# Linear attention with decay and a mixture of experts: products with the state in four quarters of TensorE, two pairs of heads exchanged

## The chip, the core and the metric

The kernel runs on one core of a Trainium2 chip. The core has five engines that work side by side: TensorE (PE, matrix products; the loads of its weights are shown as PEld), VectorE (DVE), ScalarE (ACT), GpSimd (POOL) and SyncE (SP, which here only issues loads and stores). Products land in PSUM, [...] all else lies in SBUF. The metric is the device time of one execution in microseconds; less is better.

## The reference

The first part is attention with a decaying state, for 4 sequences, 8 heads, 768 positions and a head size of 64. The second sends each of the 3072 rows of its result through the one expert of eight that a gate chooses. All data are fp32.

```python
def _attn_ref(q, k, v):
    ...
    for t in range(S):
        state = gamma[None, :, None, None] * state + np.einsum('bhd,bhe->bhde', k[:, :, t], v[:, :, t])
        y[:, :, t] = scale * np.einsum('bhd,bhde->bhe', q[:, :, t], state)
    return y.astype(np.float32)

def _moe_ref(x, w_gate, w1, w2):
    logits = x @ w_gate
    expert_idx = np.argmax(logits, axis=1)
    ...
    for e in range(E):
        ...
        h = np.maximum(x_sorted[lo:hi] @ w1[e], 0.0)
        y_sorted[lo:hi] = h @ w2[e]
    y = y_sorted[inv_perm]
    return (gate_w[:, None] * y).astype(np.float32)
```

## The kernel before

**Attention.** A sequence is cut into 6 chunks of 128 positions (two chunks of a pair hold the even and odd positions' q in one load). There are 24 steps, one for each chunk `c` and sequence `b`, in the order chunk 0 and 1 of sequence 0, then of sequence 1, and so on; then chunks 2 and 3, then 4 and 5. The decay is put into q and v by factors, so that a chunk needs only plain products. The eight heads lie in four pairs `a`; the two heads `j` of a pair lie in partitions 0 to 63 and 64 to 127.

In step n, `retain` does on TensorE:

- L440, `sc`: scores, k times q, for 8 heads. The depth is 64, so a product uses half of the array's rows and all its columns; the heads `j` alternate between the upper and the lower rows and write two banks.
- VectorE multiplies the two banks by the causal mask (L442, `am`).
- `then()`: the transposes of the next step's k (L387, 4 of them) and, for every other step, of q (8 more), which ACT copies to SBUF (L425, L428); the layout change of the step before on VectorE (L476, from `xTg` to `xg`); and one piece of the routing work.
- L451, `new`: the chunk's own contribution to the state, 8 products; VectorE adds the old state (L454).
- L465, `y`: q times the old state, 8 products of depth 64 with 64 outputs, for all chunks but the first of a sequence. The heads of a pair use the two diagonal quarters of the array: rows 0 to 63 with columns 0 to 63, and rows 64 to 127 with columns 64 to 127.
- L469, `y`: masked scores times v, added in the same place in PSUM; 8 products of depth 128 with 64 outputs, so that the two heads of a pair use the left and the right half of the columns.
- ACT copies `y` to `xTg` (L471), one copy of 128 partitions by 512.

The tile `y` has two PSUM buffers, one bank each, used in turn; `tr` has three, `sc` two, `lg` one.

**Loads.** `load(n + 5)` is issued by SyncE in step n. GpSimd scales q and v two steps ahead (L399, L404).

**Routing.** After each four steps `place` works on the 512 rows that are complete: gate products (L493, `parts`), a transpose (L502), the choice and its softmax on VectorE (L504 to L523), ranks within each expert (L526 to L540), and a list of rows for each expert (L543 to L582). `place` is a generator; the steps that follow take one piece of it at a time, in an order written out by hand. [...]

**The end of attention and the experts.** After the last step the rows of the first expert that are known already are gathered (L166), copied (L643), transposed (L656) and given to its first layer (L221). Then the eight experts follow, each with a first layer (L221, ReLU by ACT at L223) and a second one, either as plain products (L234) or, for the first 256 rows, as seven instead of eight half-size products (L275, `pair`). Outputs are scattered to HBM by GpSimd (L310).

Each fp32 product of the program appears as two matrix instructions in the trace.

## Time and profile before

| | |
|---|---|
| time, median of 3 runs | 483.25 us (480.48 to 483.81) |
| span of the profiled execution | 481.1 us |
| attention on TensorE | about 10 to 133 us |
| experts on TensorE | about 138 to 473 us |
| TensorE busy | 463.0 us (96%) |
| VectorE busy | 267.0 us (55%) |
| ScalarE busy | 106.8 us (22%) |
| GpSimd busy | 136.1 us (28%) |

Busy time counts an instruction from its start to its modelled end, and overlapping ones once. A line of a group names the line of the kernel, the engine, the operation, what it writes and reads with its shape, how often, then the busy time in us, the mean time of one in ns, and the idle time of the engine before it with what ended that. In a list in order of time the first number is the start and the second the length, both in us. The chain that ended last is followed back from the last instruction, at each point to what released it.

### The profile page before, as it was taken

The numbers are of one execution on the slowest core, as the hardware profiler recorded it, in microseconds if no ns is written. First come the engines' busy times: TensorE is split into PE (matmuls) and PEld (weight loads), VectorE is DVE, ScalarE is ACT, GpSimd is POOL, SyncE is SP. The second block draws the span as 40 slices with busy tenths as digits, with TensorE's granted clock in tenths as the row PEclk, the third lists the DMA queues.
The fourth block names the chain that finished last, engine by engine and source line by source line (L and its number), as shares of the span: only waits on it lengthen the run. The fifth ranks groups of instructions, "written<-read, shape, count | busy, mean of one in ns | idle before, by whom it ended". The sixth has DMA issues, their size and how long they took to land.

```text
span 481.1 us, 8296 instructions
## 1 busy us (share of the span) xinstructions
PE 463.0 (96%) x3262; PEld 325.1 (68%) x3262; DVE 267.0 (55%) x548; ACT 106.8 (22%) x219; POOL 136.1 (28%) x134
## 2 busy tenths in 40 slices
PE   8999999999889999999999999999999999999992
PEld 4778778787668965655585558668556765755782
DVE  4468786777677891576516632583571537470320
ACT  2343333333222011122211121131122111012110
POOL 2772533541304235023017002602601331100211
PEclk9999999999989999999999999999999999999997
DMA  9999999887831099234008401920920380240011
GB/s 204 220 236 218 216 240 221 194 209 232 278 89 41 6 354 360 115 110 164 3 28 285 169 2 53 364 80 26 354 96 32 116 350 19 66 158 3 27 46 48
DMA packets 93515, 72.53 MB, mean 151 GB/s; under 512 B 53482, under 2 KB 78058, under 8 KB 93424
## 3 DMA queue, kind: packets, MB, share of 16 engines
q1 hardware_dynamic: 88160, 58.74, 42.9%
q0 software_dynamic: 5120, 12.60, 7.5%
q8 instruction: 48, 0.79, 0.7%
q14 instruction: 43, 0.35, 0.2%
q10 hardware_dynamic: 144, 0.05, 0.0%
HBM read 60.88 MB, written 14.68 MB: 157 GB/s over the span
## 4 chain that ended last, share of the span: by engine, by line
PE 86%; DVE 7%; SPq 1%; DMA 1%; ACT 1%; issue 1%; another core or an unknown queue 1%; POOL 0%; POOLq 0%; DVEq 0%; ACTq 0%
PE hp L221 34%; PE yp L275 20%; PE ye L234 12%; PE y L469 4%; PE sc L440 4%; PE tr L387 3%; PE y L465 3%; DVE xT L209 2%; PE new L451 2%; PE parts L493 1%; DMA q<-in_q_dram 1%; SPq L374 1%; DVE am L442 1%; PE lgp L502 1%
## 5 line engine op out<-in xcount | busy, mean ns | idle before, releaser
L221 PE MATMUL hp<-xTs,w1t 128*128 128x392 f32 (+5 forms) x384 | 127.4, 493 | 0.0
L221 PEld LDWEIGHTS hp<-xTs,w1t 128*128 128x128 f32 x384 | 73.1, 190 | 52.3 <-issue 29.7
L310 POOL DMA_INDIRECT out_dram<-o,dst x30 | 33.0, 1100 | 226.5 <-ACT o L242 135.7
L209 DVE STREAM_TRANSPOSE xTs<-xs 32x512 f32<-32x512 f32 x96 | 67.4, 703 | 50.6 <-DMA xs<-x_d,src 49.3
L234 PE MATMUL ye<-w2t,hT 128*8 128x128 f32 (+6 forms) x496 | 66.4, 361 | 0.0
L223 ACT ACTIVATE hT<-hp 128x392 f32<-128x392 f32 (+6 forms) x64 | 29.4, 467 | 146.5 <-PE hp L221 130.1
L234 PEld LDWEIGHTS ye<-w2t,hT 128*8 128x8 f32 (+6 forms) x496 | 32.6, 123 | 31.3 <-issue 28.8
L166 POOL DMA_INDIRECT xs<-x_d,src x28 | 38.4, 1370 | 26.5 <-DVE gate_e L201 18.2
L442 DVE TENSOR_TENSOR am<-sc,causal 128x512 f32<-128x512 f32 x48 | 30.8, 682 | 21.7 <-PE sc L440 18.3
L281 DVE SCALAR_TENSOR_TENSOR u<-yp,gate,m 128x256 f32<-128x256 f32 x14 | 6.8, 484 | 56.2 <-PE yp L275 42.2
L404 POOL TENSOR_TENSOR vs<-v,dec 128x512 f32<-128x512 f32 x23 | 24.3, 1056 | 36.3 <-PE y L469 19.9
L275 PE MATMUL yp<-ws,hs 128*128 128x256 f32 x144 | 32.1, 380 | 0.0
L275 PEld LDWEIGHTS yp<-ws,hs 128*128 128x128 f32 x144 | 27.4, 190 | 3.7
L399 POOL TENSOR_TENSOR qs<-q,dec 128x512 f32<-128x512 f32 x22 | 22.6, 1046 | 23.6 <-DMA q<-in_q_dram 22.6
L469 PE MATMUL y<-am,vs 128*64 128x128 f32 x384 | 27.7, 279 | 1.5 <-DVE am L442 1.4
L440 PE MATMUL sc<-qT,kT 64*128 64x128 f32 x384 | 27.9, 285 | 0.7 <-ACT kT L425 0.7
L275 PE MATMUL yp<-w2t,hT 128*128 128x256 f32 x112 | 26.6, 380 | 0.0
L440 PEld LDWEIGHTS sc<-qT,kT 64*128 64x128 f32 x384 | 23.3, 187 | 4.6 <-issue 3.6
L469 PEld LDWEIGHTS y<-am,vs 128*64 128x64 f32 x384 | 21.2, 137 | 5.9 <-issue 3.3
L275 PEld LDWEIGHTS yp<-w2t,hT 128*128 128x128 f32 x112 | 21.2, 190 | 5.3 <-issue 2.8
L471 ACT COPY xTg<-y 128x512 f32<-128x512 f32 x24 | 14.1, 585 | 46.2 <-PE y L469 42.1
L221 PE MATMUL hp<-xTa,w1t 128*128 128x256 f32 (+1 forms) x128 | 22.1, 330 | 0.7 <-ACT xTa L658 0.7
(188 smaller groups left out, 543.1 us busy)
## 6 DMA issues: line engine op xcount, KB each, us to landing
w1t<-in_moe_w_dram SPq DMA_DIRECT2D x8, 2048.0 KB, 13.7
w2t<-in_moe_w_dram SPq DMA_DIRECT2D x8, 2048.0 KB, 11.6
k<-in_k_dram SPq DMA_DIRECT2D x24, 256.0 KB, 5.5
v<-in_v_dram SPq DMA_DIRECT2D x24, 256.0 KB, 5.7
x_d<-xg SPq DMA_DIRECT2D x24, 256.0 KB, 4.9
q<-in_q_dram SPq DMA_DIRECT2D x11, 512.0 KB, 5.5
q<-in_q_dram SPq DMA_DIRECT2D x2, 256.0 KB, 3.3
out_dram<-o,dst POOLq DMA_INDIRECT x30, 3.3
```

Of the source, the lines that this page charges most:

```text
L166: nc.gpsimd.indirect_dma_start(out=xs[:, t, :], out_offset=None, in_=x_d[0:rows, :], in_offset=bass.IndirectOffsetOnAxis(ap=idx[:, t : t + ...
L209: nc.vector.transpose(xT[ts(g, L), :, 0 : n * P].rearrange("p a (t r i) -> p r t a i", r=Q, i=L)[:, r, :, :, :], xs[ts(r, L), tiles[0] : t ...
L221: nc.tensor.matmul(hp, lhsT=w1t[:, 0, dt, ts(f, P)], rhs=xT[:, dt, 0:n], start=(dt == 0), stop=(dt == DT - 1))
L223: nc.scalar.activation(out=hT[:, f, 0:n], in_=hp, func=AF.Relu)
L234: nc.tensor.matmul(y[j * z : j * z + m, 0:c], lhsT=hT[:, f, t * P + r0 : t * P + r0 + m], rhs=w2t[:, 0, f, ts(j, c)], start=(f == 0), stop ...
L275: nc.tensor.matmul(y, lhsT=a[:, f, :], rhs=b[:, f, :], start=start and f == 0, stop=f == FH - 1, skip_group_check=True)
L310: done = nc.gpsimd.indirect_dma_start(out=out[:, :], out_offset=bass.IndirectOffsetOnAxis(ap=idx[:, t : t + 1], axis=0), in_=o[:, t, :], i ...
L399: mul.tensor_tensor(out=qs[:, e, part, :], in0=got["q"][:, part, ts(e, D)], in1=inner(dec[:, ts(c + e, H)][:, part], D), op=ALU.mult)
L404: mul.tensor_tensor(out=vs, in0=got["v"], in1=inner(dec[:, ts(NC + c, H)], D), op=ALU.mult)
L440: nc.tensor.matmul(sc[j][:, a, :], lhsT=kT[r, a, :], rhs=qT[r, a, :], start=True, stop=True)
L442: nc.vector.tensor_tensor(out=am[j], in0=sc[j], in1=middle(causal[:, :], HP), op=ALU.mult)
L469: nc.tensor.matmul(y[ts(j, D), a, :], lhsT=vs[:, 2 * a + j, :], rhs=am[j][:, a, :], start=(c == 0), stop=True, skip_group_check=True)
```

## The change

The exchange puts the heads of the last two pairs (a = 2, 3) on the other diagonal: the head in rows 0 to 63 writes columns 64 to 127, and the reverse. The state products of one of the first two pairs and one of the last two are issued one after the other, so that four products stand in a row that use four different quarters of the array. [...] the last two pairs have a bank of their own; both `y` buffers are now taken in each step. The second product, L469, follows the same places. The copy puts the exchanged heads back: ACT copies the first two pairs as before (128x256) and each exchanged half by itself (64x256, from the upper partitions to the lower ones and the reverse). In the last step VectorE makes these two copies.

```diff
-            y = ps("y", 2, "y").rearrange("p (a t) -> p a t", a=HP)
+
+            HB = HP // 2
+            y = [ps("y", 2, "y")[:, 0 : HB * P].rearrange("p (a t) -> p a t", a=HB) for _ in range(2)]
+            place_of = lambda a, j: y[a // HB][ts(j ^ (a // HB), D), a % HB, :]
             if c:
-                for a in range(HP):
+                for a in (0, HB, 1, HB + 1):
                     for j in range(2):
                         r = ts(j, D)
-                        nc.tensor.matmul(y[r, a, :], lhsT=old[r, a, :], rhs=qT[r, a, :], start=(a == 0), stop=False,
-                                         skip_group_check=True)
+                        nc.tensor.matmul(place_of(a, j), lhsT=old[r, a, :], rhs=qT[r, a, :], start=(a % HB == 0),
+                                         stop=False, skip_group_check=True)
             for a in range(HP):
-                for j in range(2):
-                    nc.tensor.matmul(y[ts(j, D), a, :], lhsT=vs[:, 2 * a + j, :], rhs=am[j][:, a, :], start=(c == 0),
+                for j in (range(2) if a < HB else (1, 0)):
+                    nc.tensor.matmul(place_of(a, j), lhsT=vs[:, 2 * a + j, :], rhs=am[j][:, a, :], start=(c == 0),
                                      stop=True, skip_group_check=True)
-            nc.scalar.copy(out=xTg[n // B % 2][:, :, n % B, :], in_=y)
+            x = xTg[n // B % 2][:, :, n % B, :]
+            nc.scalar.copy(out=x[:, 0:HB, :], in_=y[0])
+            for j in range(2):
+                to, got = x[ts(j, D), HB:HP, :], y[1][ts(1 - j, D), :, :]
+                if n + 1 < len(steps):
+                    nc.scalar.copy(out=to, in_=got)
+                else:
+                    nc.vector.tensor_copy(to, got)
```

## The prediction

> **What bounds the kernel now.** I read three views in this order: the page (who is busy, and the chain that ended last), the time order of one step, and VectorE's own time order around the places where its work piles up. From the page, the engine totals and the chain:

> ```profile
> PE 463.0 (96%) x3262; PEld 325.1 (68%) x3262; DVE 267.0 (55%) x548; ACT 106.8 (22%) x219; POOL 136.1 (28%) x134
> ...
> PE 86%; DVE 7%; SPq 1%; DMA 1%; ACT 1%; issue 1%; another core or an unknown queue 1%; POOL 0%; POOLq 0%; DVEq 0%; ACTq 0%
> PE hp L221 34%; PE yp L275 20%; PE ye L234 12%; PE y L469 4%; PE sc L440 4%; PE tr L387 3%; PE y L465 3%; DVE xT L209 2%; PE new L451 2%; PE parts L493 1%; DMA q<-in_q_dram 1%; SPq L374 1%; DVE am L442 1%; PE lgp L502 1%
> ```

> TensorE is 86% of the chain. The products with the state, L465, are 3%, some 15 to 20 us in the attention part (about 10 to 133 us). A microsecond saved there should reach the end: after 181 us the chain is L221, L234 and L275 in turn with no gap over 0.02 us until 472.7. One step, in time order, TensorE only (start us, us, engine, line, what):

> ```profile
> 60.66 0.66 PE L387 MATMUL tr<-ident,k 128*128 128x128 f32 x4
> 61.24 0.69 PE L451 MATMUL new<-vs,k 128*64 128x64 f32 x16
> 61.86 1.09 PE L465 MATMUL y<-qT,state 64*64 64x128 f32 x16
> 62.88 1.09 PE L469 MATMUL y<-am,vs 128*64 128x128 f32 x16
> ```

> No gap: L465 holds TensorE for 1.02 us (61.86 to 62.88), and L469 follows at once. Each product of the program is two instructions (8 give x16). Their kinds, from the groups with shapes kept apart (busy us, mean ns):

> ```profile
> L465 PE MATMUL y<-qT,state 64*64 64x128 f32 x320 | 22.1, 276 | 0.2 <-issue 0.2
> L451 PE MATMUL new<-vs,k 128*64 128x64 f32 x320 | 13.7, 228 | 0.5 <-ACT qT L428 0.5
> L234 PE MATMUL ye<-w2t,hT 128*32 128x128 f32 x128 | 3.9, 274 | 0.0
> ```

> All overlap: 276 ns each, but 22.1/320 = 69 ns apart. The third row is what the change hopes for: four tiles of the array at work at once, 128 columns streamed as in L465, and 3.9/128 = 30 ns apart.

> **How many run at once, and what a turn costs.** In the single starts of the trace L465 goes in pairs 7 ns apart, a pair every 109 ns; L234 goes in fours, one within 20 ns, a four every 109 ns. The rows agree: one burst of L465 is 22.1/20 = 1.105 us for 8 turns, one of L234 is 3.9/2 = 1.95 us for 16, so a turn is (1.95 - 1.105)/8 = 0.106 us and a burst has 0.25 us that doesn't depend on turns. I take 0.109.

> [...] L440 shows two row tiles at once, L469 two column tiles. [...] from the last start of L465 to the first of L469 is 0.20 us instead of 0.109. [...]

> **The change, part by part.**
> 1. *State products, 20 steps* (c>0, six groups of four less the first). 8 turns become 4: 20 x (8-4) x 0.109 = **8.7 us** less on TensorE. Upper price of a turn: if loading four sets of 64 weights were the limit, L451 prices it: a burst of 13.7/20 = 0.685 us, less 0.25, over 8 pairs = 0.054 per pair, so 0.109 again for four. I see no slower turn in the trace short of no overlap at all (part of the rivals).
> 2. *L469*: same 8 products, columns still alternate left, right; other banks. Nothing.
> 3. *Copies*: one ACT copy of 128x512 (585 ns) becomes one of 128x256 and two of 64x256. The nearest rows are 383 ns (the activation of 128x256) and 366 ns (L239, 64x256). The first can run beside the second half of L469, so the end of the copying moves from 0.59 to 2 x 0.37 = 0.73 us after L469; ACT is busy 0.53 us more per step, on an engine busy 8.5 of 25 us in this part. Behind them in ACT's queue stands the next kT copy, which needs L440 and the transposes first (1.09 + 0.49 = 1.6 us after L469). To L476, which reads the copies, it makes no difference: VectorE does both masks of the next step first. Nothing.
> 4. *PSUM*: both y buffers are now used in each step, so a step's first y product waits for the copies of the step before and no longer for those two back. It stands after L440, L387 and L451, at least 1.09 + 0.49 + 0.62 = 2.2 us after L469, and the copies need 0.8. Nothing; 1.4 us in hand.
> 5. *Last step*: VectorE does the two half copies, about 0.4 us each by the state row (418 ns, 128x256 out of PSUM), ahead of its copies to xe (0.72 us), while ACT copies the other half. The first two products of L493 can start earlier, the last two about 0.2 us later. I take 0; 0.3 either way for the range.

> **What keeps the 8.7 us from arriving.** L469 also needs the two masks of VectorE (L442). VectorE's time order in a step after a routing round began:

> ```profile
> 59.47 0.18 DVE L537 TENSOR_TENSOR own<-rk,ohs 128x32 f32<-128x32 f32 x1
> 59.69 0.19 DVE L540 TENSOR_REDUCE ranks<-own 128x4 int32<-128x32 f32 x1
> 59.91 0.93 DVE L543 TENSOR_SCALAR col<-ranks 128x4 int32<-128x4 int32 x1
> 60.76 0.16 DVE L544 TENSOR_SCALAR prow<-ranks 128x4 int32<-128x4 int32 x1
> 60.88 0.17 DVE L546 TENSOR_TENSOR is_col<-four,col 128x16 f32<-128x16 int32 x1
> 61.09 0.29 DVE L548 TENSOR_TENSOR at<-ohs,is_col 128x128 f32<-128x128 bf16 x1
> 61.30 1.28 DVE L442 TENSOR_TENSOR am<-sc,causal 128x512 f32<-128x512 f32 x2
> ```

> No idle time: from 53.3 (L504) to 68.8 VectorE is never free, so L442 comes when VectorE gets to it. It ends at 62.58, and L469 starts at 62.88: 0.23 us in hand, where a shorter L465 would want 0.44. [...] Going through all steps in this way (steps numbered from 0; wanted 0.44 each):
> - 1, 3, 7, 8, 11, 12, 13, 15, 16, 20, 22: L442 is done early enough. All kept.
> - 5: TensorE already waits for L442 in step 6 (40.81, 0.16 us), VectorE unbroken since 32.4. 0.44 lost.
> - 9 and 10: 0.23 kept of 0.87. 0.64 lost.
> - 14: at 88.66 TensorE waits 1.15 us for VectorE's state sum (L454), which moves only as much as its chain's start. 0.44 lost.
> - 17 to 19: L442 ends at 109.62 and L469 starts at 110.71, so about 1.03 kept of 1.31. 0.28 lost.
> - 21: the next work is L579, which needs L572, unbroken VectorE work that ends at 123.26. 0.33 lost.
> - 23: VectorE stands still from 127.50 to 130.91 before the last masks (releaser unknown to the profile); L465 is beside it. 0.44 lost.

> Lost 2.57, kept 8.7 - 2.57 = 6.1: **483.25 - 6.1 = 477.1 us**.

> Loads don't take it back: the load queue is full up to 88 us, but then waits for buffers that TensorE frees; the last v load is issued at 96.8 and lands about 5.7 us later (median), while its scaling starts at 111.95. That and all weights (w1: issued 104.3, 13.7 us to land, used at 138) have over 9 us in hand.

> **Rivals.**
> - *B, VectorE gives way too.* The piled-up stretches start when TensorE gives the routing its input[...]; if they fall elsewhere, all 8.7 arrive: 474.5. For: VectorE is busy 18.2 us of the 25 from 50 to 75 us, no full engine. Against: the unbroken stretches above.
> - *C, the quarters don't overlap fully*, because two row tiles share the output columns: 8 turns stay, 483.3. For: this trace has no four-way burst with two row tiles. Against: L440 and L234 each show half of it.
> - *D, slower: changing between the two diagonals costs a drain*[...]. Eight turns stay and three changes inside each burst cost 0.20 - 0.109, about 0.1 us each: 20 x 0.3 = 6.0, 489.2. For: the 0.20 us gap.[...]

> **How the numbers follow.** Chances: forecast 0.61, B 0.16, C 0.15, D 0.08. One per cent is 4.8 us (below 478.4). The forecast misses that in about one case of seven (its losses could be 4 us), so faster 0.52 + 0.16 = 0.68, slower 0.08, the rest same. Low end: B, less 1.5 us because L493 took 1.94 us at the reduced clock after the standstill at 130 (about 1.0 us in the earlier rounds) and L656 lost about as much; the clock may stay full: 473.0. High end 481.5: the forecast with losses doubled (479.7) and the spread of the times before (480.5 to 483.8, 1.8 us of it). D and most of C stay outside.

> **What would show it.** L465's successor at about 4 x 0.109 + 0.25 = 0.69 us per burst (13.7 us busy in all, from 22.1) and 0.58 us from its start to that of the next products; starts in fours. New waits of TensorE for L442 of 1 to 3 us in all. No wait of TensorE for ACT's y copies. If the burst stays at 1.0 us, C; above 1.2, D. If the burst is short and the waits for L442 are under 0.5 us, B.

## The result, and the profile after

| | before | changed |
|---|---|---|
| time, median (5 runs each, side by side) | 483.81 us (480.48 to 485.37) | 478.5 us (477.54 to 479.73) |
| ratio to before, 95% interval | | 0.990 (0.9856 to 0.9944) |
| span of the profiled execution | 481.1 us | 475.8 us |

The changed kernel takes 5.3 us less by the medians, and 5.3 us less by the two spans; by the interval the saving is 2.7 to 7.0 us. In the experiments further down, a run more than 1.5% above the fastest of its kernel counts as slow and is left out of the medians and ranges. From here on the lines of the changed kernel are meant where it is spoken of: L468 are its products with the state (L465 before), L472 the masked ones (L469), L475 and L479 ScalarE's copies (L471), L481 VectorE's two copies of the last step, L486 the layout change (L476). All of the routing stands ten lines lower than before.

The page of the changed kernel, engine totals and chain:

```profile
PE 456.0 (96%) x3262; PEld 316.9 (67%) x3262; DVE 267.2 (56%) x550; ACT 118.5 (25%) x265; POOL 135.9 (29%) x134
...
PE 83%; DVE 7%; DMA 4%; SPq 1%; issue 1%; ACT 1%; another core or an unknown queue 1%; POOL 0%; POOLq 0%; DVEq 0%; ACTq 0%
PE hp L221 34%; PE yp L275 20%; PE ye L234 12%; PE y L472 4%; PE sc L440 3%; DMA w2t<-in_moe_w_dram 3%; PE tr L387 3%; PE new L451 2%; PE y L468 2%; DVE am L442 2%; PE parts L503 1%; DMA q<-in_q_dram 1%; SPq L374 1%; PE lgp L512 1%
```

TensorE is 7.0 us less busy with the same 3262 instructions, and the products with the state fall from 3% of the chain to 2%. VectorE's masks, L442, rise from 1% to 2%: part of the gain meets them. ScalarE has 46 instructions more and 11.7 us more to do. The new 3% of a load of second-layer weights (w2t) is hardly a loss: at 175 us TensorE waits 1.1 us for it, where before it waited 0.95 us for VectorE.

The same kernel, TensorE, time order of the step that was shown of before (start us, us, engine, line, what), and the groups of this part with shapes kept apart:

```profile
57.08 0.66 PE L387 MATMUL tr<-ident,k 128*128 128x128 f32 x4
57.66 0.69 PE L451 MATMUL new<-vs,k 128*64 128x64 f32 x16
58.28 0.67 PE L468 MATMUL y<-qT,state 64*64 64x128 f32 x16
58.87 1.09 PE L472 MATMUL y<-am,vs 128*64 128x128 f32 x16
```

```profile
L472 PE MATMUL y<-am,vs 128*64 128x128 f32 x384 | 29.5, 285 | 1.3 <-DVE am L442 1.2
L468 PE MATMUL y<-qT,state 64*64 64x128 f32 x320 | 13.8, 282 | 1.9 <-issue 1.2 <-remote 0.7
L451 PE MATMUL new<-vs,k 128*64 128x64 f32 x320 | 13.7, 228 | 0.5 <-ACT qT L428 0.5
```

One product takes as long as before (282 ns against 276), but the sixteen now hold TensorE for 0.67 us instead of 1.09, and L472 starts 0.60 us after L468 (58.28 to 58.87) instead of 1.02. So the gain is overlap, not shorter instructions. The last row is a control: L451 was not touched, and kept its 13.7 us and 228 ns. L472 has 29.5 us, L469 had 27.7: the last burst of L472 takes 2.48 us, while the granted clock of TensorE is 0.5 (from 125.5 to 128.9 us). The trace of before has such a stretch too, from 133.7 to 137.1 us, so the two traces are alike in this.

The waits of TensorE in the attention part, 10 to 135 us (engine, line, waited for: us in total, times, longest), changed kernel:

```profile
PE y L472 <- DVE am L442: 1.2, 3, 0.8
PE y L468 <- issue: 1.2, 1, 1.2
PE tr L387 <- DVE state L454: 1.2, 1, 1.2
PE tr L387 <- POOL qs L399: 0.8, 2, 0.4
PE y L468 <- remote: 0.7, 1, 0.7
PE hp L221 <- ACT xTa L668: 0.7, 1, 0.7
PE found L589 <- DVE here L582: 0.6, 1, 0.6
```

In the trace of before the waits for masks came to 1.4 us, 1.2 of them in the last step. The total says little, then; what is new is 1.0 us in step 17.

**Where the time went.** The start of the masked products, compared step by step between the two traces, tells how far the changed kernel is ahead. It starts 0.69 us ahead in step 0, which the change did not bring: up to 7.4 us the first transposes of q on TensorE (L387) follow each other after 0.21 us in the trace of before, and after 0.11 us here. The loads landed alike (the first scaling of q starts at 4.05 and 4.04 us).

```
step                1     5     8     9    14    15    16    17    18    19    21    22    23
ahead, us        0.88  1.72  2.59  3.69  5.71  7.20  7.63  7.17  7.00  6.03  6.73  6.44  6.01
```

Each of the 20 bursts should add 0.42 us (1.02 - 0.60), 8.4 us in all. Steps 9 and 15 add more: there the kernel before had waited (0.83 us at L526 and 1.15 us for L454), and the changed one does not; that gives 1.75 us above the 0.42. Steps 17 to 19 lose: instead of adding 1.26 they take 1.60 (7.63 to 6.03), 2.9 us short. Steps 21 to 23 are 1.7 us short and step 1 is 0.24 short; the remaining steps add up to -0.06. Thus 8.4 + 1.75 - 2.9 - 1.7 - 0.24 - 0.06 = 5.3 us, or 6.0 with the head start.

The lead is 6.3 us when the experts begin and 6.2 after the first of them. At 330.43 us L221 starts after a gap of 0.68 us, and from there to the end the lead is 5.3. The two pages show the gap, before first:

```profile
L221 PE MATMUL hp<-xTs,w1t 128*128 128x392 f32 (+5 forms) x384 | 127.4, 493 | 0.0
L221 PE MATMUL hp<-xTs,w1t 128*128 128x392 f32 (+5 forms) x384 | 127.5, 493 | 0.7 <-issue 0.7
```

"issue" means that TensorE waited for nothing that the profile shows. All ten traces of kernels with the exchange have this gap, 0.5 to 1.2 us long; the three of kernels without it don't. Its cause is not known, and VectorE's masks have no part in it.

The 1.75 us of steps 9 and 15 are chance and not the change: the kernel of the second set that has no exchange is 1.76 us faster than the trace of before in the same two steps. So the sum of 5.3 us holds some 4.9 us of losses in the attention part, which luck made good in part.

What holds steps 17 to 19 is VectorE. Its time order there in the changed kernel:

```profile
91.77 0.19 DVE L526 TENSOR_REDUCE idx<-top 128x4 f32<-128x32 f32 x1
91.99 0.79 DVE L528 TENSOR_TENSOR ohs<-em,idx 128x32 bf16<-128x32 f32 x1
92.70 0.17 DVE L531 TENSOR_REDUCE gate<-ex 128x4 f32<-128x32 f32 x1
92.91 0.85 DVE L532 TENSOR_SCALAR gate<-gate 128x4 f32<-128x4 f32 x1
93.79 0.18 DVE L533 RECIPROCAL gate<-gate 128x4 f32<-128x4 f32 x1
93.89 1.26 DVE L442 TENSOR_TENSOR am<-sc,causal 128x512 f32<-128x512 f32 x2
```

And TensorE beside it:

```profile
93.13 0.67 PE L468 MATMUL y<-qT,state 64*64 64x128 f32 x16
94.60 0.43 PE L472 MATMUL y<-am,vs 128*64 128x128 f32 x2 [0.81 <-DVE am L442]
95.20 1.09 PE L472 MATMUL y<-am,vs 128*64 128x128 f32 x14 [0.17 <-DVE am L442]
```

L528 and L532 take 0.79 and 0.85 us for work that took 0.19 and 0.17 us in the trace of before, and VectorE has no idle time before the masks. The first mask ends at 94.55, and TensorE, done with L468 0.8 us earlier, stands still for it. Two steps later L387 waits 1.2 us for the state sum (L454), again behind VectorE's queue. In step 22 TensorE waits 0.6 us for VectorE's lists (L589). In step 23 both kernels wait for the masks behind a standstill of VectorE of 3.4 us, so the shorter burst isn't kept there.

Beside it GpSimd, in the changed kernel, and then in the kernel before:

```profile
91.69 2.04 POOL L399 TENSOR_TENSOR qs<-q,dec 128x512 f32<-128x512 f32 x2 [2.74 <-DMA q<-in_q_dram]
```

```profile
93.09 2.04 POOL L399 TENSOR_TENSOR qs<-q,dec 128x512 f32<-128x512 f32 x2
97.70 1.04 POOL L404 TENSOR_TENSOR vs<-v,dec 128x512 f32<-128x512 f32 x1 [2.56 <-PE y L469]
```

The scaling of q (L399) waits for its load, and came only 1.4 us earlier than before (93.09 to 91.69). The choice of the experts on VectorE, which TensorE feeds, came 7.6 us earlier (its L528 stood at 99.61 before as L518, and now at 91.99). So it ran into the scaling: both long instructions start within its 91.69 to 93.73, while before the scaling was over at 95.13. The repeat of the changed kernel shows the same (L399 at 91.97, long instructions at 92.15 and 93.32). In all, GpSimd waits longer for q than before, as the two pages show (before first):

```profile
L399 POOL TENSOR_TENSOR qs<-q,dec 128x512 f32<-128x512 f32 x22 | 22.6, 1046 | 23.6 <-DMA q<-in_q_dram 22.6
L399 POOL TENSOR_TENSOR qs<-q,dec 128x512 f32<-128x512 f32 x22 | 22.5, 1043 | 36.3 <-DMA q<-in_q_dram 35.1
```

Long instructions of this kind lie beside a scaling in all 13 traces. The 0.93 us of L543 that the prediction's list shows (0.17 elsewhere) is one case: L404 runs beside it for 1.04 us from 59.78. Take the kinds of VectorE instruction whose median is at most 0.3 us. Up to 126 us they take more than 0.5 us 123 times. Each of these lies beside a scaling of GpSimd (L399 or L404) and ends 0.01 to 0.15 us after one ends. Of the 1324 with no scaling beside them none is that long (158 of them are in the two traces of the result, the longest 0.32 us), and reductions (L526 and L531 are two) are never lengthened: in the two traces of the result 34 of these kinds lie beside a scaling, and they take 0.17 to 0.29 us. No run took the scaling away, so it is a coincidence without exception and not a test.

There are 10 such long instructions in the trace of before and 9 in that of the changed kernel. The change did not add to them but moved them: the two waits of before in steps 9 and 15 followed such instructions as well (0.96 and 0.98 us at 54.21 and 55.21, 0.94 to 0.98 us from 84.37 on).

### The profile page after: what moved, and what is told of

It reads as the page before. It is cut to its first block, busy times and chain, and to the rows that moved or that the text cites. A ratio compares the mean times of both kernels' runs of the same rounds, so it can differ in the third digit from the quotient of the medians.

```text
span 475.8 us, 8355 instructions
## 1 busy us (share of the span) xinstructions
PE 456.0 (96%) x3262; PEld 316.9 (67%) x3262; DVE 267.2 (56%) x550; ACT 118.5 (25%) x265; POOL 135.9 (29%) x134
## 3 DMA queue, kind: packets, MB, share of 16 engines
HBM read 60.88 MB, written 14.68 MB: 159 GB/s over the span
## 4 chain that ended last, share of the span: by engine, by line
PE 83%; DVE 7%; DMA 4%; SPq 1%; issue 1%; ACT 1%; another core or an unknown queue 1%; POOL 0%; POOLq 0%; DVEq 0%; ACTq 0%
PE hp L221 34%; PE yp L275 20%; PE ye L234 12%; PE y L472 4%; PE sc L440 3%; DMA w2t<-in_moe_w_dram 3%; PE tr L387 3%; PE new L451 2%; PE y L468 2%; DVE am L442 2%; PE parts L503 1%; DMA q<-in_q_dram 1%; SPq L374 1%; PE lgp L512 1%
## 5 line engine op out<-in xcount | busy, mean ns | idle before, releaser
L221 PE MATMUL hp<-xTs,w1t 128*128 128x392 f32 (+5 forms) x384 | 127.5, 493 | 0.7 <-issue 0.7
L221 PEld LDWEIGHTS hp<-xTs,w1t 128*128 128x128 f32 x384 | 73.0, 190 | 53.3 <-issue 30.9
L209 DVE STREAM_TRANSPOSE xTs<-xs 32x512 f32<-32x512 f32 x96 | 67.5, 703 | 50.6 <-DMA xs<-x_d,src 49.3
L234 PE MATMUL ye<-w2t,hT 128*8 128x128 f32 (+6 forms) x496 | 66.4, 361 | 0.0
L234 PEld LDWEIGHTS ye<-w2t,hT 128*8 128x8 f32 (+6 forms) x496 | 32.6, 123 | 31.4 <-issue 28.8
L166 POOL DMA_INDIRECT xs<-x_d,src x28 | 38.3, 1369 | 26.2 <-DVE gate_e L201 18.0
L442 DVE TENSOR_TENSOR am<-sc,causal 128x512 f32<-128x512 f32 x48 | 30.7, 682 | 18.1 <-PE sc L440 14.6
L399 POOL TENSOR_TENSOR qs<-q,dec 128x512 f32<-128x512 f32 x22 | 22.5, 1043 | 36.3 <-DMA q<-in_q_dram 35.1
L275 PE MATMUL yp<-ws,hs 128*128 128x256 f32 x144 | 32.1, 380 | 0.0
L472 PE MATMUL y<-am,vs 128*64 128x128 f32 x384 | 29.5, 285 | 1.3 <-DVE am L442 1.2
L275 PEld LDWEIGHTS yp<-ws,hs 128*128 128x128 f32 x144 | 27.4, 190 | 3.7
L404 POOL TENSOR_TENSOR vs<-v,dec 128x512 f32<-128x512 f32 x23 | 24.1, 1050 | 17.9 <-DMA v<-in_v_dram 11.3
L440 PE MATMUL sc<-qT,kT 64*128 64x128 f32 x384 | 27.9, 285 | 0.7 <-ACT kT L425 0.7
L472 PEld LDWEIGHTS y<-am,vs 128*64 128x64 f32 x384 | 22.6, 140 | 6.1 <-DVE am L442 3.1
L275 PE MATMUL yp<-w2t,hT 128*128 128x256 f32 x112 | 26.6, 380 | 0.0
L440 PEld LDWEIGHTS sc<-qT,kT 64*128 64x128 f32 x384 | 23.3, 188 | 4.6 <-issue 3.6
L275 PEld LDWEIGHTS yp<-w2t,hT 128*128 128x128 f32 x112 | 21.2, 190 | 5.3 <-issue 2.8
L221 PE MATMUL hp<-xTa,w1t 128*128 128x256 f32 (+1 forms) x128 | 22.1, 330 | 0.7 <-ACT xTa L668 0.7
L221 PE MATMUL hp<-xT,w1t 128*128 128x392 f32 x64 | 21.3, 494 | 1.1 <-DMA w2t<-in_moe_w_dram 1.1
## 6 DMA issues: line engine op xcount, KB each, us to landing
w1t<-in_moe_w_dram SPq DMA_DIRECT2D x8, 2048.0 KB, 13.8
```

Source lines behind the costliest of these rows:

```text
L166: nc.gpsimd.indirect_dma_start(out=xs[:, t, :], out_offset=None, in_=x_d[0:rows, :], in_offset=bass.IndirectOffsetOnAxis(ap=idx[:, t : t + ...
L209: nc.vector.transpose(xT[ts(g, L), :, 0 : n * P].rearrange("p a (t r i) -> p r t a i", r=Q, i=L)[:, r, :, :, :], xs[ts(r, L), tiles[0] : t ...
L221: nc.tensor.matmul(hp, lhsT=w1t[:, 0, dt, ts(f, P)], rhs=xT[:, dt, 0:n], start=(dt == 0), stop=(dt == DT - 1))
L234: nc.tensor.matmul(y[j * z : j * z + m, 0:c], lhsT=hT[:, f, t * P + r0 : t * P + r0 + m], rhs=w2t[:, 0, f, ts(j, c)], start=(f == 0), stop ...
L275: nc.tensor.matmul(y, lhsT=a[:, f, :], rhs=b[:, f, :], start=start and f == 0, stop=f == FH - 1, skip_group_check=True)
L399: mul.tensor_tensor(out=qs[:, e, part, :], in0=got["q"][:, part, ts(e, D)], in1=inner(dec[:, ts(c + e, H)][:, part], D), op=ALU.mult)
```

## The experiments

The runs were made on two chips; times are compared only with runs of the kernel before in the same set. The ratio beside a time is the recorded estimate with its 95% interval, not the quotient of the two medians. The first theory was: four products that stand in a row and use four quarters start together; their turn of 0.109 us is the whole gain; VectorE's queue takes part of it back. The rivals: the two banks (a bank is here the place of one PSUM tile of the program, 128x512 fp32) or the smaller copies give the gain; loads, or the exchange of the columns, take it back.

### First set (kernel before: 482.96 us, median of 34 runs)

**The changed kernel again**, as a measure for the others.

> The changed kernel again, so that the other runs of this set can be set beside it. Both theories: 478.5 us or within 1.5 of it, L468 bursts of 0.60 us up to L472.

Measured 479.24 us, ratio 0.9932 (0.9899 to 0.9965). The gain stands, at 3.7 us. In its trace too a late mask stops TensorE in step 17 (1.55 us from L468 to L472); in the steps before it L472 always follows after 0.60 us. Step 18 then takes 6.08 us, 1.6 more than in the trace of the result; the granted clock is 0.5 from 96.8 to 100.2 us.

**The same products in the order of the pairs**, so that no four in a row use four quarters:

```diff
-                for a in (0, HB, 1, HB + 1):
+                for a in range(HP):
```

> The changed kernel with the state products in the order of the pairs 0, 1, 2, 3, so that only one diagonal at a time has work; exchange, second bank and divided copies stay. Theory 1 (the gain is the four turns saved per burst): the burst is 1.0 us again and the time that of before, 483.8 +- 1.5. Rival 2 (the gain comes from the second bank or from copies that start earlier): under 480. Rival 3 (the exchange costs time of its own, which the changed kernel gains back): over 486.

Measured 479.27 us, 0.9923 (0.9894 to 0.9952): no loss at all. The first theory failed here, and the time alone is what the rival of the bank and the copies foretold (under 480 us). This kernel's group of state products:

```profile
L468 PE MATMUL y<-qT,state 64*64 64x128 f32 x320 | 14.2, 282 | 1.7 <-issue 1.2 <-ACT xTg L479 0.5
```

14.2 us as against 13.8: four turns, not eight. How it does this can be read from the single starts of one burst (us; first and second turn):

```
changed:   58.276 58.283 58.289 58.296    58.436 58.443 58.449 58.456
in order:  59.338 59.345 59.365 59.371    59.498 59.505 59.525 59.531
```

The changed kernel's four follow at 0, 7, 13 and 20 ns, about 6.7 ns for each product. In order, they follow at 0, 7, 27 and 33 ns, which is 0, 1, 4 and 5 times 6.7 ns. Products 4 and 5 of the program are the first that use the other diagonal. The reading that fits: TensorE takes a product every 6.7 ns or so, a product whose quarter is busy waits at that quarter, and the ones behind it still start. The trace doesn't say which product a start belongs to. But had the products been put in another order ahead of the chip, four starts without a hole would be expected, as in the changed kernel.

**Small routing work moved to GpSimd**, in both kernels: the parts of the gate told to the table (`told`, `less`, `val`) and the lists (`here`) for the first groups, which VectorE does otherwise. This takes work from VectorE alone, and changes nothing on TensorE.

```diff
+            eng = nc.gpsimd if c < NC - 2 else nc.vector
-                nc.vector.tensor_copy(told[:, g0 : g0 + B, i], part)
+                eng.tensor_copy(told[:, g0 : g0 + B, i], part)
...
-                    nc.vector.tensor_tensor(out=less, in0=part, in1=told[:, g0 : g0 + B, i], op=ALU.subtract)
+                    eng.tensor_tensor(out=less, in0=part, in1=told[:, g0 : g0 + B, i], op=ALU.subtract)
...
-            nc.vector.tensor_tensor(out=val, op=ALU.mult, in1=inner(told[:, g0 : g0 + B, :], E * TC), in0=bass.AP(
+            eng.tensor_tensor(out=val, op=ALU.mult, in1=inner(told[:, g0 : g0 + B, :], E * TC), in0=bass.AP(
...
-                nc.vector.tensor_scalar(out=here[:, b, :], in0=rrow, scalar1=prow[:, b : b + 1], scalar2=None,
+                eng.tensor_scalar(out=here[:, b, :], in0=rrow, scalar1=prow[:, b : b + 1], scalar2=None,
```

In the changed kernel:

> The changed kernel, with the small routing operations on told, less, val and here of the first four groups on GpSimd instead of VectorE (about 2.4 us of VectorE work per group). Theory 1 (VectorE's piled-up work holds back L472 and L387): TensorE's waits for L442, L454 and L582 shrink from 3 us to under 1 and the time falls by 1.5 to 3 us, to 475.5 to 477. Rival 2 (the missing part is lost elsewhere, at the standstill near 121 us and the load of weights): within 1 us of the changed kernel. Rival 3 (GpSimd becomes the bound, it waits for q loads): slower by 1 us or more.

In the kernel before:

> The same move of small routing operations to GpSimd in the kernel before. Theory 1: TensorE waited for VectorE only some 3 us there, so 481 to 482.5; the changed kernel with the move is then 6 to 7.5 us faster than this, more than the 5.3 between the two without it. Rival 2: the difference stays 5.3 or less. Rival 3: slower than before.

Measured: 476.29 us, 0.9865 (0.9804 to 0.9926), in the changed kernel; 483.59 us, 0.9993 (0.9952 to 1.0033), in the one before. VectorE's relief is worth 3.0 us where the products are short (479.24 to 476.29) and nothing where they are long, against my expectation of a gain there too. So the quarters give 7.3 us with VectorE relieved (483.59 - 476.29), of the 8.4 they take from TensorE, and 3.7 without. The ranges of the relieved and the changed kernel just overlap (475.46 to 478.07 and 477.87 to 483.09 us). The changed kernel with the relief, waits of TensorE in the attention part:

```profile
PE y L472 <- DVE am L442: 0.6, 3, 0.2
```

The longest wait for a mask fell from 0.8 to 0.2 us, and the wait for L454 is gone. The waits for L442, L454 and the lists come to 1.2 us instead of 3.0 (under 1 was expected), and one of 0.7 us for L528 is new. Busy time of the engines between 50 and 75 us (stretch, length, then PE, PEld, DVE, ACT, POOL with their instructions, clock, DMA), the changed kernel first and the relieved one second:

```profile
50.00:75.00 25.00, 24.67 (x388) 20.01 (x386) 19.64 (x58) 12.27 (x29) 12.99 (x13) 1.00 1.07 234
```

```profile
50.00:75.00 25.00, 24.51 (x384) 19.80 (x380) 17.33 (x48) 12.40 (x29) 16.76 (x24) 1.00 1.03 232
```

GpSimd takes longer than VectorE for the larger of these operations (`here` 603 ns against 246, `val` 1.26 us against 0.83), and the kernel gains from the move all the same. Of the long instructions on VectorE, this trace has 6 and that of the relief in the third set 4, against 9, 8 and 14 in the three of the changed kernel.

### Second set, another chip (kernel before: 480.26 us, median of 35 runs)

**VectorE makes both half copies in every step**: more work where the theory says it hurts.

```diff
-                if n + 1 < len(steps):
+                if n < 0:
```

> The changed kernel, but VectorE makes the two copies of the exchanged heads in every step, not only in the last (0.86 us more on VectorE per step, 0.74 less on ACT). Theory 1 (VectorE's order is what takes part of the gain): TensorE waits for L442 in many steps and the whole gain goes: 483 to 490 us. Rival 2 (VectorE has room, what is lost is lost at the end of attention): within 1.5 us of the changed kernel, 479.

Measured 484.17 us, 1.0073 (1.0045 to 1.0101): slower than the kernel before by 3.9 us, though the state products still take their short 14.0 us. Its waits, in an execution of 486.64 us, the longest of its 11 runs:

```profile
PE y L472 <- DVE am L442: 4.2, 6, 2.2
PE tr L387 <- DVE state L454: 2.3, 2, 1.9
```

The two copies take VectorE 0.86 us a step. The same burst on TensorE can thus win 4 us or lose 4, by what VectorE has to do; this run and the relief show it in both directions.

**The gathers for the first expert later in the program.** In the first traces VectorE stands still for 3.4 us ahead of the last masks, and the suspicion was on the gathers (L166) that run near it.

```diff
-                for e in range(2):
-                    gather(xs2[e], src[:, e * TC :], range(HALF), (c + 1) * B * P)
-                early.extend([head, far])
+                early.extend([head, far, src, (c + 1) * B * P])
...
+        src, rows = early[2:]
+        for e in range(2):
+            gather(xs2[e], src[:, e * TC :], range(HALF), rows)
+        early[2:] = []
```

> The changed kernel, with the four first gathers (L166, with src_e) issued after the last step instead of in step 22. If the gathers make VectorE, ACT and TensorE stand still near 121 us, the 3.4 us before the last masks goes and L472 of step 23 starts some 2 us earlier; if the stillness has another cause (an instruction fetch is in both traces at its start), it stays. The time as a whole is no verdict: xe then waits for gathers that start some 5 us later, so 478 to 484.

Measured 475.77 us, 0.9898 (0.9845 to 0.9951). It tells little: GpSimd had nothing else ahead, so the gathers ran from 120.4 us on, 1.4 us ahead of the masked products of step 22, as in the changed kernel's trace. The standstill was absent all the same. The traces of the result's two kernels and all four of the first set have it; the seven from the second chip, this one among them, don't (L468 to L472 of the last step 0.94 us here, 2.01 us in the changed kernel's trace of the result). So it goes with the chip or its state, and not with the order of the gathers. The instruction fetch named in the expectation starts where the standstill does, at 127.5 us in the trace of before (VectorE idle from 127.50) and at 121.3 in that of the changed kernel (from 121.47), which is all the traces show of it. The cause stays open.

**Own bank and split copy, no exchange**: the last two pairs keep their diagonal.

```diff
-            place_of = lambda a, j: y[a // HB][ts(j ^ (a // HB), D), a % HB, :]
+            place_of = lambda a, j: y[a // HB][ts(j, D), a % HB, :]
...
-                for j in (range(2) if a < HB else (1, 0)):
+                for j in range(2):
...
-            for j in range(2):
-                to, got = x[ts(j, D), HB:HP, :], y[1][ts(1 - j, D), :, :]
-                if n + 1 < len(steps):
-                    nc.scalar.copy(out=to, in_=got)
-                else:
-                    nc.vector.tensor_copy(to, got)
+            nc.scalar.copy(out=x[:, HB:HP, :], in_=y[1])
```

> The last two pairs of heads keep their own bank, but are not exchanged: the state products use one diagonal of the array, in the order of the changed kernel, and ACT makes two copies of 128x256. Theory 1 (four quarters at once save four turns of 0.109 us): 8 turns, 1.0 us from L468 to L472, and the time of before, 483.5 +- 1.5. Rival 2 (the gain comes from the second bank or from copies that start earlier): under 480.5.

Measured 480.02 us, 1.0006 (0.9981 to 1.0031). The state products of this kernel:

```profile
L468 PE MATMUL y<-qT,state 64*64 64x128 f32 x320 | 21.8, 276 | 0.0
```

21.8 us, as before the change (22.1), with the bank, the split copy and the interleaved order all in place. The bank and the copies give nothing; what the exchange adds to them is the whole gain. And no wait for L442 is listed for TensorE: with long bursts, and without the standstill of the last step, the masks are in time.

**All upper heads, then all lower ones**, the furthest order from four in a row:

```diff
-                for a in (0, HB, 1, HB + 1):
-                    for j in range(2):
+                for j in range(2):
+                    for a in range(HP):
```

> The changed kernel with the four products of the upper rows issued first and then the four of the lower rows, so that the third and fourth quarter stand four products back in the queue. If TensorE lets products of a free quarter start ahead of products that wait for a busy one, as the run in the order of the pairs suggests: 4 turns again, 0.60 us from L468 to L472 and 479 us. If it looks only two products ahead: 6 to 8 turns, 0.8 to 1.0 us, and 480.5 to 483.5 us.

Measured 476.03 us, 0.9886 (0.9845 to 0.9928). Its state products:

```profile
L468 PE MATMUL y<-qT,state 64*64 64x128 f32 x320 | 13.7, 282 | 0.0
```

Four turns again. The starts of a turn stand at 61.880, 61.894, 61.907 and 61.920 us: 0, 14, 27 and 40 ns, or 0, 2, 4 and 6 times 6.7 ns. By the program products 0, 2, 4 and 6 are the first ones of the four quarters. The reading made from the order of the pairs thus foretold this one.

### Third set, on the second chip (kernel before: 480.34 us, median of 27 runs)

**One more group of lists on GpSimd**, besides the relief above:

```diff
-                eng.tensor_scalar(out=here[:, b, :], in0=rrow, scalar1=prow[:, b : b + 1], scalar2=None,
+                (nc.gpsimd if c < NC - 1 else nc.vector).tensor_scalar(out=here[:, b, :], in0=rrow, scalar1=prow[:, b : b + 1], scalar2=None,
```

> The changed kernel with the small routing operations on GpSimd as before, and the comparisons for here (L582) of the fifth group too, for which TensorE still waited 0.6 us in step 21. Theory 1: the wait for here goes, 0.3 to 0.6 us less than the run without this, so 1.4 to 1.7% under the kernel before. If GpSimd's slower comparisons (603 ns instead of about 200) come later than VectorE's did, the same as without or up to 1 us more.

**The relief again**, as in the first set:

> The run with the small routing operations on GpSimd once more, beside the two others of this set on one chip: 1.3% under the kernel before (0.985 to 0.990), and 2 to 3 us under the changed kernel.

**The changed kernel again:**

> The changed kernel once more on the chip of this set: 0.989 to 0.994 of the kernel before. On a chip whose step 23 has no standstill, L468 of step 23 keeps its 0.42 us as well.

Measured: with one more group 477.11 us (472.27 to 479.05, 17 runs), 0.9924 (0.9896 to 0.9953); the relief 474.17 us (473.02 to 474.87, 6 runs), 0.9851 (0.9805 to 0.9897); the changed kernel 476.6 us (475.26 to 479.51, 10 runs), 0.9912 (0.987 to 0.9954). The relief is again the fastest, by 2.4 us over the changed kernel (3.0 in the first set). The intervals overlap, but all its runs lie below all runs of the changed kernel. It beats the kernel before by 6.2 us. The further group is inconclusive: its runs spread over 6.8 us, and its profiled execution, 472.27 us, was the fastest. The wait that it should remove was not gone in it (0.8 us at L590). What spreads its times was not found.

The changed kernel's trace here loses in other steps than that of the result. In step 6 TensorE waits 1.9 us for a mask, and then the granted clock is 0.5 from 41.8 to 45.2 us: steps 6 and 7 lose 3.4 us, steps 17 to 19 only 1.6. In step 23 the 0.42 us are not kept, though without the standstill they were expected to be: L472 waits 0.27 and 0.10 us for masks and follows L468 after 0.94 us.

## Why the prediction was right, and where it was off

- **The size of the gain on TensorE was right.** The forecast was four turns of 0.109 us less for each burst, 8.7 us; the trace shows 0.42 us a burst, 8.4 us. 0.58 us from L468 to L472 was forecast and 0.60 measured; 13.7 us busy forecast, 13.8 measured. The turn was worked out from pairs and from one short four-way row. The small rest has its place too: the last product of a turn now starts 20 ns into it instead of 7, which takes 0.013 us back in each burst.
- **Rivals C and D are ruled out.** Two row tiles on the same columns do overlap (four starts within 20 ns), and changing between the diagonals costs nothing that shows (turns of 0.109 us, as before). In the trace of before, the two row tiles of L440 and the two column tiles of L469 start 6 to 7 ns apart. **B** is ruled out as it was put: 8.4 us do not all arrive, and the waits for L442 are 1.2 us, not below 0.5. B was right that VectorE's piled-up stretches fall elsewhere; they cost as much there. With VectorE relieved in both kernels, 7.3 of the 8.4 arrive: nearly B's case, but only by a further change.
- **The copies cost nothing, as costed.** ScalarE's copies take 372 and 366 ns (taken: 383 and 366). L468 did wait once for the y copies where none was forecast:

```profile
PEld y L468 <- ACT xTg L479: 0.9, 1, 0.9
```

  This is the load of weights of the last step, during the standstill; both buffers of y were in use. The masks came later still (the first ended at 125.59 us, L472 started at 125.74), so it cost nothing.
- **The term that was off is the loss, 2.57 us.** By the result's traces it is 3.1 us (8.4 less 5.3). That the two are so near is luck: 4.9 us are lost in the attention part, the trace of before happened to lose 1.75 there, and the head start and the gap at 330 us, which no one forecast, nearly cancel. The two repeats have more runs and save 3.7 us each, which makes the loss 4.7. In the repeats a part of it is no wait at all but TensorE at half the granted clock (96.8 to 100.2 and 41.8 to 45.2 us), which the forecast had only at the end of attention. Of the 1.4 us between 477.1 forecast and 478.5 measured, 0.8 is the smaller saving (6.1 against 5.3), and 0.6 the kernel before, which had 483.81 us in these runs instead of 483.25.
- **Its places were mostly wrong.** Losses were forecast for step 5 (0.44 us), for 9 and 10 (0.64) and for 14 (0.44). Only 0.06 us was lost at the first of these and nothing at the others, and 1.75 us came on top as two waits of the trace of before fell away. For steps 17 to 19 the forecast was 0.28 us, and 2.9 were lost. For 21 to 23 it was 0.77 (0.33 and 0.44), and 1.7 were lost. The forecast took VectorE's instructions with the lengths of the trace of before, and what it says of the loads looks at the last load of v and at the weights, not at when GpSimd's work on a load of q falls. The loads kept their pace up to 90 us while TensorE gained 7 on them, and GpSimd's work on a load then lay beside VectorE's small instructions. A small slip: from 62.58 to 62.88 us is 0.30 us, of which the forecast took 0.23 without saying why.
- **One assumption was not needed**: that four products for different quarters must stand in a row. Two orders without that keep the four turns (14.2 and 13.7 us busy, against 13.8) and save as much. Nor does TensorE start the products of a burst in the order of the program, as the starts are read here (0, 7, 27 and 33 ns in the one, 0, 14, 27 and 40 ns in the other). The ends are modelled in these traces, so nothing is said about them.

## What to carry to other kernels

When small products use half of TensorE's rows and half of its columns, look for a layout in which all four quarters have work in the same burst (here those that share columns wrote separate PSUM banks, and one bank for both was not run); the order in the program mattered little within a burst of eight (13.8, 14.2 and 13.7 us busy in three orders). Then read which engine feeds the products that follow, and how much it has in hand: the burst gave 8.4 us here, and between -3.9 and +7.3 us arrived, depending on what VectorE had to do. Relieve that engine in the same change, and don't expect the relief to pay by itself beforehand. And don't trust a list of steps made from one trace: where the waits fell changed from one execution to the next.
